# A Strassen down-projection over pairs of 512-token chunks

## The chip, the core and the metric

One NeuronCore of one Trainium2 chip runs the whole kernel. The metric is the device time of one launch in microseconds (us), the median of three runs. Engines are named as in the profile: PE (TensorE, matrix multiply; PEld is its loading of weights), DVE (VectorE), ACT (ScalarE), POOL (GpSimd) and SP (SyncE, which only issues DMAs). Each engine runs its own instructions in the order in which the program lists them (the schedule is manual for all five), and waits on semaphores for the others.

## What is computed

```python
def _attn_ref(u, v, z):                      # u, v: 8 x 3008 x 256; z: 8 x 3008 x 64
    scores = (1.0 / S) * np.matmul(z, z.transpose(0, 2, 1))
    attn = np.maximum(scores, 0.0) ** 2
    return (u * np.matmul(attn, v)).astype(np.float32)

def _moe_ref(x, w_in, w_out):                # x: 24064 x 256, the rows of the above
    h = x @ w_in                             # 256 x 2048
    g = h * (1.0 / (1.0 + np.exp(-1.702 * h)))
    return (g @ w_out).astype(np.float32)    # 2048 x 256
```

An attention without softmax, gated by u, and then a feed-forward layer: an up-projection to 2048, a Gelu by sigmoid, a down-projection to 256.

## The kernel before

The batch loop has eight rounds. In each, the 3008 tokens form six chunks: five of 512, and a last one of 448. Of two successive batches the even one keeps only 384 tokens of its last chunk for the feed-forward, and its other 64 join the odd one's, which is then 512 wide (`blocks`).

**Attention.** For each query chunk `i`, `attend` yields some 47 steps; each is a pair of 64-row matmuls of 512 columns (or one of 128 rows), which accumulate `V` times the squared scores in two PSUM banks (L367). Between steps `take` emits score matmuls (L235), an ACT Relu (L256) and a DVE square into a tile of tag `a` (26 buffers, L270) for a later chunk; during the last query chunk these belong to the next batch. Some squares are also transposed by DMA on SP (`turn_unit`, L298) into tiles of tag `tt` (14 buffers). Those of the next batch's first chunk are put off in the list `late`. When a query chunk is done, DVE multiplies by `u` and leaves `XT`, 256 features by 512 tokens in float16.

**Up-projection.** `up_group(b, q)` makes 256 of the 2048 hidden rows for one chunk: four matmuls of 512 columns (L408) into an `hg` tile (two PSUM buffers), a Gelu on ACT (L416) into `gf` (two buffers), and a scaling into float16 `GT` (tag `tt`) on DVE (L420), or, where `q % 8` is 1, 3 or 5 and `q` is 16 or more, on ACT (L418). A chunk has eight groups, a batch 48. The first 16 are emitted between the steps of a query chunk (the fifth; in the last batch the sixth), the other 32 after attention, each followed by one product of the down-projection. The products that are left (10 or 11) follow without up groups.

**Down-projection.** It is a Strassen-Winograd product within a chunk. The left matrix is `GT`, split by hidden rows (0 to 1023 and 1024 to 2047) and by tokens (even and odd blocks of 128): a11, a12 are the even blocks, a21, a22 the odd ones. The right matrix is `w_out`, split into four, with its sums t1 to t4n made once on DVE. The left sums S1 = a21 + a22, S2 = S1 - a11, S3 = a11 - a21 (in place of a21), S4 = a12 - S2 are made on DVE (L479 to L488); they wait in the list `SUMS`, of which each up group, after its scaling, emits one (two if more than eight wait). `product` emits one of seven products: eight matmuls of 256 columns (L532). There are three PSUM banks for a chunk, of the four of tag `ps1`: P1, P6, P7 and P4 add up in the first, P5 and P3 in the second, P2 has the third. What is read from a bank before the next product adds into it goes to `y`, either as an ACT copy (L549) or as a DVE addition (L553):

```python
lst += [(k, "P1")] + ([(k - 1, "P4"), (k - 1, "P3")] if k else []) + one   # one: P6 P5 P7 P2
...
copy = {"P1": (0, 0), "P6": (0, 1), "P7": (1, 1), "P4": (1, 0)}
outs = {"P2": (0, 0, "P2"), "P7": (1, 1, "P5"), "P3": (0, 1, "P5")}
```

Where a chunk has only 384 tokens, its Strassen part is 256 of them, so its matmuls have 128 columns, and the last 128 tokens are done by plain matmuls (`odd_block`, L506). In the last two chunks of the last batch `rows(b, k)` swaps the operands, so that tokens come out as rows (L535).

**Store.** When a chunk is done, `store` transposes `y` on DVE (L589) into `yo` (one buffer) and SP issues four DMAs (L599). The last two chunks of a batch are stored during the next one (`LAST2`). `y` has two buffers.

**Weights of the first layer.** In batch 0, `w_in` is loaded in four quarters by POOL (`load_w`) and cast by ACT (`cast_w`, L452) at places given by the tables `LOADW` and `CASTW`: keys are (query chunk, step), values the quarter. Quarter k holds up groups 2k and 2k + 1.

Of the kernel before, what the change touches and what calls it, by code (L numbers as in the profile page):

```python
# [9 lines left out]
F32 = mybir.dt.float32  # L10
F16 = mybir.dt.float16
P = 128
# [3 lines left out]
def kernel(  # L16
# [13 lines left out]
    AF = mybir.ActivationFunctionType  # L30
    ALU = mybir.AluOpType

    B, S, D = u.shape
# [20 lines left out]
    FSC = csc * csc * float(S) * float(S)  # L54
# [23 lines left out]
    late, LATE = [], []  # L78
# [316 lines left out]
    GT, Y = {}, {}  # L395

    def blocks(b):

        return [(i, CH if i < NCH - 1 or b % 2 else LFULL) for i in range(NCH)]

    def up_group(b, q):
        k, fg = divmod(q, NFG)
        i, n = blocks(b)[k]
        hg = ps2.tile([P, FFG, CH], F32, name="hg", tag="ps2")
        for e in range(FFG):
            ff = fg * FFG + e
            for c in range(NCC):
                pe.matmul(  # L408
                    hg[:, e, :n], W1[:, c, ff * P:(ff + 1) * P], XT[b, i][:, c, :n],
                    start=(c == 0), stop=(c == NCC - 1),  # L410
                )
        if fg % 2 == 0:
            GT[b, k, fg // 2] = pa.tile([P, CB, CH], F16, name="gt", tag="tt", bufs=14)
        g = GT[b, k, fg // 2][:, (fg % 2) * FFG:(fg % 2 + 1) * FFG, :n]
        gf = pw.tile([P, FFG, CH], F32, name="gf", tag="gf")
        act.activation(gf[:, :, :n], hg[:, :, :n], AF.Gelu_apprx_sigmoid, scale=1.0 / FSC)  # L416
        if q >= LAGY and q % 8 in (1, 3, 5):
            act.activation(g, gf[:, :, :n], AF.Copy, scale=FSC)  # L418
        else:
            dve.tensor_scalar(g, gf[:, :, :n], FSC, None, ALU.mult)  # L420
        for s_ in [SUMS.pop(0) for _ in range(min(len(SUMS), 1 + (len(SUMS) > 8)))]:
            s_()
        if fg in (NFG - 3, NFG - 1):
            SUMS.extend(left_sums(b, k, fg == NFG - 1))


# [11 lines left out]

    def load_w(k):

        if k < 2:
            hold = const.tile([P, 1], F16, name=f"hold{k}")
            pool.tensor_copy(hold, XT[0, k + 1][:, 0, :1])
# [46 lines left out]
    def products(b):  # L490

        lst = []
        for k in range(NCH):
            one = [(k, "P6"), (k, "P5"), (k, "P7"), (k, "P2")]
            if blocks(b)[k][1] < CH:
                one.insert(0, (k, "odd"))
            lst += [(k, "P1")] + ([(k - 1, "P4"), (k - 1, "P3")] if k else []) + one
        return lst + [(k, "P4"), (k, "P3")]

    def odd_block(b, k):  # L500

        s = blocks(b)[k][1] // P - 1
        yp = ps1.tile([P, NCC, P], F32, name="yp", tag="ps1")
        for c in range(NCC):
            for ff in range(NFF):
                pe.matmul(  # L506
                    yp[:, c, :], W2K[:, ff, c], GT[b, k, ff // CB][:, ff % CB, s * P:(s + 1) * P],
                    start=c == 0 and ff == 0, stop=ff == NFF - 1, skip_group_check=True,
                )
        act.activation(Y[b, k][:, :, s * P:(s + 1) * P], yp, AF.Copy, scale=1.0 / FSC)  # L510

    def product(b, k, name):
        if name == "odd":
            odd_block(b, k)
            return
        mm = pairs(b, k)
        right = {
            "P1": W2K[:, LO, 0], "P2": W2K[:, HI, 0], "P3": W2K[:, HI, 1], "P4": WT[:, 3],
            "P5": WT[:, 0], "P6": WT[:, 1], "P7": WT[:, 2],
        }[name]  # L520
        if name in ("P1", "P2", "P5"):
            ST[b, k, "bank" + name] = ps1.tile([P, 2, P], F32, name="st", tag="ps1")
        bank = ST[b, k, "bank" + {"P6": "P1", "P7": "P1", "P4": "P1", "P3": "P5"}.get(name, name)][:, :mm]
        for ff in range(NFF // 2):
            h, f = divmod(ff, CB)
            lhs = {
                "P1": lambda: left(b, k, h, 0), "P2": lambda: left(b, k, h + 2, 0),
                "P4": lambda: left(b, k, h + 2, 1),
            }.get(name) or (lambda: ST[b, k, {"P3": "S4", "P5": "S1", "P6": "S2", "P7": "S3"}[name], h])
            first, last = name in ("P1", "P2", "P5") and ff == 0, ff == NFF // 2 - 1  # L530
            if not rows(b, k):
                pe.matmul(bank, right[:, ff], lhs()[:, f], start=first, stop=last, skip_group_check=True)  # L532
                continue
            for m in range(mm):
                pe.matmul(  # L535
                    bank[:, m], lhs()[:, f, m], right[:, ff],
                    start=first and m == 0, stop=last, skip_group_check=True,
                )
        if name == "P1":
            Y[b, k] = pw.tile([P, NCC, CH], F32, name="y", tag="y")  # L540

        if rows(b, k):
            y = Y[b, k].rearrange("p e x -> p (e x)").rearrange("p (o m t k) -> p k m o t", o=2, t=P, k=NCC)
        else:
            y = Y[b, k].rearrange("p k (m o t) -> p k m o t", o=2, t=P)[:, :, :mm]
        copy = {"P1": (0, 0), "P6": (0, 1), "P7": (1, 1), "P4": (1, 0)}
        if name in copy:
            o, c = copy[name]
            act.activation(y[:, c, :, o], bank, AF.Copy, scale=1.0 / FSC)  # L549
        outs = {"P2": (0, 0, "P2"), "P7": (1, 1, "P5"), "P3": (0, 1, "P5")}  # L550
        if name in outs:
            o, c, x = outs[name]
            dve.scalar_tensor_tensor(  # L553
                y[:, c, :, o], ST[b, k, "bank" + x][:, :mm], 1.0 / FSC, y[:, c, :, o], ALU.mult, ALU.add,
            )
        if rows(b, k):
            if name in ("P4", "P3"):
                store_rows(b, k, name == "P4")
        elif name == "P3" and k > NCH - 3 and b < B - 1:
            LAST2.append(lambda: store(b, k))  # L560
        elif name == "P3":
            store(b, k)
# [21 lines left out]
    def store(b, k):  # L584

        i, n = blocks(b)[k]
        r0, m = b * S + i * CH, n // QW
        yo = pw.tile([P, CH // QW, QW, NCC], F32, name="yo", tag="yo", bufs=1)
        dve.transpose(  # L589
            yo[:, :m].rearrange("p q c k -> p q k c"), Y[b, k][:, :, :n].rearrange("p k (q t) -> p q k t", t=QW),  # L590
        )
        parts = [(r0, 0, n)]
        if n > S - i * CH:
            full = S0 - i * CH
            parts = [(r0, 0, full)] + [((b - h) * S + S0, full + h * SREM, SREM) for h in range(2)]
# [11 lines left out]
    def pieces(b, i):  # L607
# [22 lines left out]
    LOAD0 = {(1, 14): 2, (2, 12): 3, (2, NJ + 20): 4, (4, 8): 5}  # L630
    TURN = {(1, NJ + 4): 2, (2, NJ + 4): 3, (4, NJ + 4): 4, (5, 8): 5}
    LOADW = {
        (2, 16): 0, (3, 0): 1, (3, 9): 2, (3, 41): 3, (4, 28): 4, (4, 34): 5, (4, 40): 6, (5, 0): 7,
    }
    CASTW = {(3, 8): 0, (3, 40): 1, (4, 8): 2, (4, 14): 3}
    LOAD = {(3, NJ + 20): 4, (4, NJ + 5): 5}

    FIRST_ZT, FIRST_CAST = {12: 4, 20: 5}, {5: 4, 13: 5}
# [46 lines left out]
    for b in range(B):  # L685
# [47 lines left out]
        for q in range(head, nup):  # L733
            if more and q in (head + 14, head + 20):
                k = int(q == head + 20)
                turn_u(b + 1, k)
                load_u(b + 1, k + 2)
            up_group(b, q)
            if b == 0 and q == head + 3:
                wsums.pop(0)()  # L740
            product(b, *prods.pop(0))
            if q >= 30 and q % 2 and late:
                late.pop(0)[1]()
        steps = [lambda kp=kp: product(b, *kp) for kp in prods]
# [41 lines left out]
```

## Time and profile before

| what | value |
|---|---|
| runs | 1179.65 us median (1179.23 to 1181.85) |
| span of the profiled execution, first to last instruction | 1177.7 us (its time around the span is not given) |
| PE busy | 1171.1 us, 9284 matmuls |
| PE weight loads busy | 670.1 us, 9284 loads |
| DVE, ACT busy | 870.9 us, 849.7 us |
| POOL busy | 208.0 us |
| matmuls of the up-projection (L408) | 1536 |
| matmuls of the Strassen products (L532; L535) | 2576; 224 |
| plain matmuls of the odd blocks (L506) | 128 |

The profile is of one execution. A group's line gives the line of the code, the engine, the operation, the tiles written and read, the shape, the count, then busy time and the mean duration of one in ns, then the idle time of the engine before them and what ended it. Matmuls are pipelined: the duration of one runs from its start to the end of its results, and the next starts earlier. A timeline's line has start and duration in us; an x8 after it means that eight like instructions are merged.

### The profile page before, as it was taken

What the parts mean: (1) busy time and instruction counts of PE and PEld (TensorE: products, weight loads), DVE (VectorE), ACT (ScalarE), POOL (GpSimd) and SP (SyncE); (2) the same over time, 40 slices, a digit from 0 to 9 for tenths busy, and PEclk for the clock granted to TensorE, in tenths of its full rate; (3) what the DMA queues carried; (4) which work ended last, traced back from release to release, by engine and by line L of the source; (5) the groups of instructions that cost most, each with busy time, mean ns of one, the idle gap of its engine ahead of it and who ended that gap; (6) DMA issues with size and microseconds to landing.
All of it is one profiled execution on the core that took longest, in us unless ns stands there. A gap on an engine that the chain in (4) does not pass through costs nothing.

```text
span 1177.7 us, 23588 instructions
## 1 busy us (share of the span) xinstructions
PE 1171.1 (99%) x9284; PEld 670.1 (57%) x9284; DVE 870.9 (74%) x1455; ACT 849.7 (72%) x1033; POOL 208.0 (18%) x294
## 2 busy tenths in 40 slices
PE   9999999999999999999999999999999999999998
PEld 3546764466644675446654467544674446744566
DVE  6788875778757786587875878658786587764776
ACT  7888874688646887478864787657876578772785
POOL 3033101231012310133101430014200241001000
PEclk9999999999999999999999999999999999999999
DMA  9998679866797678966779668795678955797023
GB/s 221 207 141 123 134 114 160 94 108 135 117 148 97 108 137 129 146 97 94 147 121 146 103 93 155 125 151 92 98 134 142 136 104 97 126 157 129 1 37 73
DMA packets 459039, 143.65 MB, mean 122 GB/s; under 512 B 424624, under 2 KB 453040, under 8 KB 458928
## 3 DMA queue, kind: packets, MB, share of 16 engines
q1 hardware_dynamic: 402464, 102.36, 53.1%
q0 software_dynamic: 55104, 38.49, 21.5%
q8 instruction: 72, 1.18, 0.4%
q10 hardware_dynamic: 1360, 1.31, 0.3%
q14 instruction: 39, 0.32, 0.1%
HBM read 60.29 MB, written 24.64 MB: 72 GB/s over the span
## 4 chain that ended last, share of the span: by engine, by line
PE 99%; ACT 1%; DVE 0%; issue 0%
PE o L367 40%; PE hg L408 28%; PE st L532 23%; PE sc L235 6%; PE st L535 1%; PE yp L506 1%; PE w L99 0%; ACT rl L256 0%; ACT W L452 0%; ACT gf L416 0%; PE zp L135 0%; ACT ZT L143 0%; DVE a L270 0%; DVE zst L128 0%; DVE y L553 0%
## 5 line engine op out<-in xcount | busy, mean ns | idle before, releaser
L416 ACT ACTIVATE gf<-hg 128x1024 f32<-128x1024 f32 (+1 forms) x384 | 385.4, 1004 | 113.7 <-PE hg L408 98.7
L256 ACT ACTIVATE rl<-sc 128x1024 f16<-128x1024 f32 (+1 forms) x301 | 287.4, 993 | 144.6 <-PE sc L235 100.4
L367 PEld LDWEIGHTS <-V 64*128 64x128 f16 (+1 forms) x4098 | 219.7, 94 | 251.4 <-issue 9.3
L408 PE MATMUL hg<-xt,W 128*128 128x512 f16 (+1 forms) x1408 | 354.6, 374 | 0.2
L367 PE MATMUL o<-a,V 64*128 64x512 f16 (+3 forms) x2278 | 296.1, 368 | 0.3 <-DVE a L270 0.3
L420 DVE TENSOR_SCALAR gt<-gf 128x1024 f16<-128x1024 f32 (+1 forms) x288 | 200.2, 695 | 114.0 <-ACT gf L416 113.5
L270 DVE TENSOR_TENSOR a<-rl 128x1024 f16<-128x1024 f16 (+1 forms) x266 | 178.3, 674 | 112.0 <-ACT rl L256 110.0
L195 POOL DMA_DIRECT2D uq<-in_u_dram x168 | 110.7, 666 | 738.4 <-PE sc L235 529.0
L367 PE MATMUL o<-tt,V 64*128 64x512 f16 (+1 forms) x1518 | 232.5, 377 | 0.0
L408 PEld LDWEIGHTS <-W 128*128 128x128 f16 x1536 | 149.4, 98 | 125.5 <-issue 2.6
L532 PEld LDWEIGHTS <-WT 128*128 128x128 f16 x1472 | 139.1, 98 | 45.1
L532 PEld LDWEIGHTS <-W 128*128 128x128 f16 x1104 | 104.7, 98 | 32.2
L235 PE MATMUL sc<-ZT 64*128 64x512 f16 (+3 forms) x688 | 115.6, 356 | 0.6 <-ACT ZT L143 0.3
L418 ACT ACTIVATE gt<-gf 128x1024 f16<-128x1024 f32 (+1 forms) x96 | 98.9, 1030 | 3.0
L549 ACT ACTIVATE y<-st 128x256 f32<-128x256 f32 x192 | 70.7, 368 | 35.6 <-PE st L532 29.0
L532 PE MATMUL st<-gt,WT 128*128 128x256 f16 (+1 forms) x736 | 91.9, 268 | 0.0
L532 PE MATMUL st<-gt,W 128*128 128x256 f16 (+1 forms) x736 | 90.8, 268 | 0.0
L532 PE MATMUL st<-s,WT 128*128 128x256 f16 (+1 forms) x736 | 90.8, 268 | 0.0
L553 DVE SCALAR_TENSOR_TENSOR y<-st,y 128x256 f32<-128x256 f32 (+1 forms) x144 | 57.7, 408 | 24.6 <-ACT y L549 11.5
L384 DVE TENSOR_TENSOR xt<-o,ut 128x512 f16<-128x512 f32 x80 | 51.4, 683 | 28.5 <-PE o L367 28.5
L486 DVE TENSOR_TENSOR s<-s,gt 128x1024 f16<-128x1024 f16 (+1 forms) x96 | 65.6, 683 | 1.1
L484 DVE TENSOR_TENSOR s<-gt 128x1024 f16<-128x1024 f16 (+1 forms) x96 | 64.7, 674 | 0.0
(59 smaller groups left out, 670.3 us busy)
## 6 DMA issues: line engine op xcount, KB each, us to landing
out_dram<-yo SPq DMA_DIRECT2D x156, 128.0 KB, 2.8
uq<-in_u_dram POOLq DMA_DIRECT2D x140, 128.0 KB, 3.3
V<-in_v_dram POOLq DMA_DIRECT2D x35, 256.0 KB, 6.3
tt<-a SPq DMA_TRANSPOSE x232, 3.4
uq<-in_u_dram POOLq DMA_DIRECT2D x28, 112.0 KB, 4.5
out_dram<-yo SPq DMA_DIRECT2D x28, 96.0 KB, 7.1
uq<-in_u_dram SPq DMA_DIRECT2D x20, 128.0 KB, 4.2
wst<-in_moe_w_in_dram POOLq DMA_DIRECT2D x4, 512.0 KB, 5.8
```

What stands on the lines that cost most here:

```text
L195: eng.dma_start(uq[k * QW:(k + 1) * QW, :n // QW].rearrange("t q c k -> t q (c k)"), src[:, :, cs])
L235: pe.matmul(sc[:, r, :q1 - q0], zt[h, 2 * kp + r, :], zt[h].rearrange("d n p -> d (n p)")[:, q0:q1], start=True, stop=True,)
L256: act.activation(rl[:, :, :n], sc[:, :, :n], AF.Relu, scale=csc)
L270: dve.tensor_tensor(a[:, :, :n], rl[:, :, :n], rl[:, :, :n], ALU.mult)
L367: ins = pe.matmul(acc[c][:, :n], V16[b][h, j].rearrange("p (c k) -> p k c", k=NCC)[:, c], weights(b, i, j)[h], start=(k, m) == first[c], s ...
L408: pe.matmul(hg[:, e, :n], W1[:, c, ff * P:(ff + 1) * P], XT[b, i][:, c, :n], start=(c == 0), stop=(c == NCC - 1),)
L416: act.activation(gf[:, :, :n], hg[:, :, :n], AF.Gelu_apprx_sigmoid, scale=1.0 / FSC)
L418: act.activation(g, gf[:, :, :n], AF.Copy, scale=FSC)
L420: dve.tensor_scalar(g, gf[:, :, :n], FSC, None, ALU.mult)
L486: dve.tensor_tensor(s_, ST[b, k, "S1", h], a11, ALU.subtract)
L532: pe.matmul(bank, right[:, ff], lhs()[:, f], start=first, stop=last, skip_group_check=True)
L549: act.activation(y[:, c, :, o], bank, AF.Copy, scale=1.0 / FSC)
```

## The change

The Strassen split by tokens now takes two neighbouring chunks: a11, a12 are chunk 2s, a21, a22 chunk 2s + 1. All three pairs are formed in batches 0 to 6; in batch 7 the third pair is left as it was, with `product` (`paired`). In the third pair of an even batch the width `w` is 384, and the 128 tokens that chunk 4 has beyond that go to `odd_block`.

- The up groups of a pair are interleaved: 16 groups in the order of `TILES`, each hidden group first for one chunk, then for the other. A `GT` tile holds one hidden group of both chunks.
- `pair_product` emits a product in two halves of four matmuls of up to 512 columns, one half after each up group. P5 is now copied by ACT and P7 added by DVE.
- The order of the halves is a list; for the third pair another one. 32 halves stand after up groups as 32 products did, and 10 or 11 steps follow.
- `pair_sum` makes the left sums by hidden group. S1, S2, S3 of a group are put into `SUMS` two groups after its a11, S4 three groups after.
- Stores: chunk 2s when P2 is done, chunk 2s + 1 two steps after P4 (`AFTER`); those of the third pair go to `LAST2`.
- `late` is emitted from q = 44 on at each group, no longer from q = 30 at each odd one.
- Quarters 1 and 2 of `w_in` change places in `LOADW` and `CASTW`.

```diff
+    TILES = (0, 4, 1, 5, 2, 6, 3, 7)
     def up_group(b, q):
-        k, fg = divmod(q, NFG)
+        s, r = divmod(q, 2 * NFG)
+        pair = paired(b, s)
+        if pair:
+            fg, e = TILES[r // 2], r % 2
+            if fg >= NFG // 2:
+                e = 1 - e
+            k = 2 * s + e
...
+            if r % 2 == 0:
+                GT[b, s, fg, "pair"] = pa.tile([P, FFG, 2, CH], F16, name="gt", tag="tt", bufs=14)
+            g = GT[b, s, fg, "pair"][:, :, k % 2, :n]
...
+        if pair:
+            some = {2: ("S1", "S2", "S3"), 3: ("S4",)}.get(r % 4, ())
+            SUMS.extend([lambda m=m, fg=fg: pair_sum(b, s, fg - NFG // 2, m) for m in some])
...
+            if s < NCH // 2 - 1:
+                order = ["P1", "P1", "P5", "P5", "P6", "P6", "P3", "P3", "P7", "P7", "P2", "P2", "P4", "P4"]
+            else:
+                order = ["P1", "P1", "P5", "P2", "P5", "P2", "P6", "P6", "P3", "P3", "P7", "P7", "P4", "P4"]
+                if blocks(b)[2 * s + 1][1] < CH:
+                    order[6:6] = ["odd"]
...
+        for ff in range(half * NFF // 4, (half + 1) * NFF // 4):
+            m, f = divmod(ff, FFG)
+            while name in form and (b, s, form[name], m) not in ST:
+                SUMS.pop(0)()
+            lhs = pair_part(b, s, raw[name])(m) if name in raw else ST[b, s, form[name], m]
+            pe.matmul(
+                bank, right[:, ff], lhs[:, f], start=new and ff == 0, stop=ff == NFF // 2 - 1, skip_group_check=True,
+            )
...
+        copy = {"P1": (0, 0), "P5": (1, 1), "P6": (0, 1), "P4": (1, 0)}
+        outs = {"P3": (0, 1), "P7": (1, 1), "P2": (0, 0)}
...
+        elif name == "P2" and not last:
+            store(b, 2 * s)
+        elif name == "P4":
+            AFTER.append([2, lambda: store(b, 2 * s + 1)])
...
-        (2, 16): 0, (3, 0): 1, (3, 9): 2, (3, 41): 3, (4, 28): 4, (4, 34): 5, (4, 40): 6, (5, 0): 7,
+        (2, 16): 0, (3, 0): 2, (3, 9): 1, (3, 41): 3, (4, 28): 4, (4, 34): 5, (4, 40): 6, (5, 0): 7,
...
-    CASTW = {(3, 8): 0, (3, 40): 1, (4, 8): 2, (4, 14): 3}
+    CASTW = {(3, 8): 0, (3, 40): 2, (4, 8): 1, (4, 14): 3}
...
-            if q >= 30 and q % 2 and late:
+            if q >= 44 and late:
                 late.pop(0)[1]()
```

More of the change, by code (lines that the diff above doesn't have):

```diff
@@ L399, in blocks, with paired @@
         return [(i, CH if i < NCH - 1 or b % 2 else LFULL) for i in range(NCH)]
+    def paired(b, s):
+        return b < B - 1 or s < NCH // 2 - 1
+    TILES = (0, 4, 1, 5, 2, 6, 3, 7)
     def up_group(b, q):
-        k, fg = divmod(q, NFG)
+        s, r = divmod(q, 2 * NFG)
[6 more added lines that the diff above has]
+        else:
+            k, fg = divmod(q, NFG)
         i, n = blocks(b)[k]
@@ L411, in up_group @@
                 )
-        if fg % 2 == 0:
-            GT[b, k, fg // 2] = pa.tile([P, CB, CH], F16, name="gt", tag="tt", bufs=14)
-        g = GT[b, k, fg // 2][:, (fg % 2) * FFG:(fg % 2 + 1) * FFG, :n]
+        if pair:
+            if r % 2 == 0:
+                GT[b, s, fg, "pair"] = pa.tile([P, FFG, 2, CH], F16, name="gt", tag="tt", bufs=14)
+            g = GT[b, s, fg, "pair"][:, :, k % 2, :n]
+        else:
+            if fg % 2 == 0:
+                GT[b, k, fg // 2] = pa.tile([P, CB, CH], F16, name="gt", tag="tt", bufs=14)
+            g = GT[b, k, fg // 2][:, (fg % 2) * FFG:(fg % 2 + 1) * FFG, :n]
         gf = pw.tile([P, FFG, CH], F32, name="gf", tag="gf")
@@ L422, in up_group @@
             s_()
-        if fg in (NFG - 3, NFG - 1):
+        if pair:
+            some = {2: ("S1", "S2", "S3"), 3: ("S4",)}.get(r % 4, ())
+            SUMS.extend([lambda m=m, fg=fg: pair_sum(b, s, fg - NFG // 2, m) for m in some])
+        elif fg in (NFG - 3, NFG - 1):
             SUMS.extend(left_sums(b, k, fg == NFG - 1))
@@ L439, in load_w @@
     def load_w(k):
-        if k < 2:
+        if k in (0, 2):
             hold = const.tile([P, 1], F16, name=f"hold{k}")
-            pool.tensor_copy(hold, XT[0, k + 1][:, 0, :1])
+            pool.tensor_copy(hold, XT[0, 1 + k // 2][:, 0, :1])
         if k < 4:
@@ L492, in products, with pair_part, pair_sum, odd_block @@
         lst = []
[L493 to L502, printed above, removed]
+        for s in range(NCH // 2):
+            if not paired(b, s):
+                continue
+            if s < NCH // 2 - 1:
+                order = ["P1", "P1", "P5", "P5", "P6", "P6", "P3", "P3", "P7", "P7", "P2", "P2", "P4", "P4"]
+            else:
+                order = ["P1", "P1", "P5", "P2", "P5", "P2", "P6", "P6", "P3", "P3", "P7", "P7", "P4", "P4"]
+                if blocks(b)[2 * s + 1][1] < CH:
+                    order[6:6] = ["odd"]
+            lst += [lambda s=s, m=m, h=order[:x].count(m): pair_product(b, s, m, h) for x, m in enumerate(order)]
+        if not paired(b, NCH // 2 - 1):
+            k = NCH - 2
+            names = [(k, m) for m in ("P1", "P6", "P5", "P7", "P2")] + [(k + 1, "P1"), (k, "P4"), (k, "P3")]
+            names += [(k + 1, m) for m in ("P6", "P5", "P7", "P2", "P4", "P3")]
+            lst += [lambda k=k, m=m: product(b, k, m) for k, m in names]
+        return lst
+    def pair_part(b, s, name):
+        f, e = {"a11": (0, 0), "a12": (1, 0), "a21": (0, 1), "a22": (1, 1)}[name]
+        w = blocks(b)[2 * s + 1][1]
+        return lambda m: GT[b, s, f * NFG // 2 + m, "pair"][:, :, e, :w]
+    def pair_sum(b, s, m, name):
+        a11, a12, a21, a22 = (pair_part(b, s, x)(m) for x in ("a11", "a12", "a21", "a22"))
+        if name == "S3":
+            ST[b, s, name, m] = a21
+            dve.tensor_tensor(a21, a11, a21, ALU.subtract)
+            return
+        s_ = pa.tile([P, FFG, CH], F16, name="s", tag="a", bufs=26)
+        s_ = ST[b, s, name, m] = s_[:, :, :blocks(b)[2 * s + 1][1]]
+        if name == "S1":
+            dve.tensor_tensor(s_, a21, a22, ALU.add)
+        elif name == "S2":
+            dve.tensor_tensor(s_, ST[b, s, "S1", m], a11, ALU.subtract)
+        else:
+            dve.tensor_tensor(s_, a12, ST[b, s, "S2", m], ALU.subtract)
+    def odd_block(b, s):
+        k, w = 2 * s, blocks(b)[2 * s + 1][1]
         yp = ps1.tile([P, NCC, P], F32, name="yp", tag="ps1")
@@ L506, in odd_block @@
                 pe.matmul(
-                    yp[:, c, :], W2K[:, ff, c], GT[b, k, ff // CB][:, ff % CB, s * P:(s + 1) * P],
+                    yp[:, c, :], W2K[:, ff, c], GT[b, s, ff // FFG, "pair"][:, ff % FFG, 0, w:w + P],
                     start=c == 0 and ff == 0, stop=ff == NFF - 1, skip_group_check=True,
                 )
-        act.activation(Y[b, k][:, :, s * P:(s + 1) * P], yp, AF.Copy, scale=1.0 / FSC)
+        act.activation(Y[b, k][:, :, w:w + P], yp, AF.Copy, scale=1.0 / FSC)
@@ new lines, in pair_product @@
+    def pair_product(b, s, name, half):
+        if name == "odd":
+            odd_block(b, s)
+            return
+        w = blocks(b)[2 * s + 1][1]
+        right = {
+            "P1": W2K[:, LO, 0], "P2": W2K[:, HI, 0], "P3": W2K[:, HI, 1], "P4": WT[:, 3],
+            "P5": WT[:, 0], "P6": WT[:, 1], "P7": WT[:, 2],
+        }[name]
+        raw = {"P1": "a11", "P2": "a12", "P4": "a22"}
+        form = {"P3": "S4", "P5": "S1", "P6": "S2", "P7": "S3"}
+        new = name in ("P1", "P2", "P5")
+        if new and half == 0:
+            ST[b, s, "bank" + name] = ps1.tile([P, CH], F32, name="st", tag="ps1")
+        bank = ST[b, s, "bank" + {"P6": "P1", "P7": "P1", "P4": "P1", "P3": "P5"}.get(name, name)][:, :w]
+        for ff in range(half * NFF // 4, (half + 1) * NFF // 4):
[6 more added lines that the diff above has]
+            )
+        if half == 0:
+            return
+        for e, at in ((0, "P1"), (1, "P5")):
+            if name == at:
+                Y[b, 2 * s + e] = pw.tile([P, NCC, CH], F32, name="y", tag="y")
+        copy = {"P1": (0, 0), "P5": (1, 1), "P6": (0, 1), "P4": (1, 0)}
+        outs = {"P3": (0, 1), "P7": (1, 1), "P2": (0, 0)}
+        e, c = copy.get(name) or outs[name]
+        y = Y[b, 2 * s + e][:, c, :w]
+        if name in copy:
+            act.activation(y, bank, AF.Copy, scale=1.0 / FSC)
+        else:
+            dve.scalar_tensor_tensor(y, bank, 1.0 / FSC, y, ALU.mult, ALU.add)
+        last = s == NCH // 2 - 1
+        if name == "P4" and last:
+            LAST2.extend([lambda: store(b, 2 * s), lambda: store(b, 2 * s + 1)])
+        elif name == "P2" and not last:
+            store(b, 2 * s)
+        elif name == "P4":
+            AFTER.append([2, lambda: store(b, 2 * s + 1)])
@@ L512, in product @@
+    AFTER = []
     def product(b, k, name):
-        if name == "odd":
-            odd_block(b, k)
-            return
         mm = pairs(b, k)
@@ L740 @@
                 wsums.pop(0)()
-            product(b, *prods.pop(0))
-            if q >= 30 and q % 2 and late:
+            prods.pop(0)()
+            for a_ in AFTER:
+                a_[0] -= 1
+            while AFTER and AFTER[0][0] < 0:
+                AFTER.pop(0)[1]()
+            if q >= 44 and late:
                 late.pop(0)[1]()
-        steps = [lambda kp=kp: product(b, *kp) for kp in prods]
+        steps = prods
         for step in steps:
```

## The prediction

> **What bounds the kernel now.** I read the page first: busy times, the clock row, the chain.
>
> ```profile
> PE 1171.1 (99%) x9284; PEld 670.1 (57%) x9284; DVE 870.9 (74%) x1455; ACT 849.7 (72%) x1033; POOL 208.0 (18%) x294
> ...
> PEclk9999999999999999999999999999999999999999
> ...
> PE 99%; ACT 1%; DVE 0%; issue 0%
> ```
>
> TensorE (PE) is idle for 6.6 us of a span of 1177.7 us, at full clock, and the chain is PE nearly from end to end. PE waits for almost nobody, so there are two ways to change the time: matmul time taken away, or a wait of PE that was not there.
>
> Second, the groups by shape, for the price of a matmul.
>
> ```profile
> L408 PE MATMUL hg<-xt,W 128*128 128x512 f16 x1280 | 328.6, 379 | 0.2
> L532 PE MATMUL st<-gt,WT 128*128 128x256 f16 x672 | 87.1, 273 | 0.0
> L506 PE MATMUL yp<-gt,W 128*128 128x128 f16 x128 | 7.8, 219 | 0.0
> ```
>
> The mean of one (379, 273, 219 ns) is its latency, not its price, since matmuls overlap. The price is the distance between neighbouring starts in the trace: 215.9 ns for 512 columns (mean of 1056), 109.2 ns for 256 (2100), 55.8 for 128, 162.5 for 384 (L408 on the short chunk). So a column costs 0.417 ns and a matmul some 2.5 ns besides. A 512-column matmul ends 379 - 216 = 0.163 us after the next one could start; 384 columns give the same 0.163.
>
> Third, the timeline of the last up groups of a batch (b = 3); q counts up groups, q = 44 starts at 579.84, q = 47 at 585.05. Columns: start, duration.
>
> ```profile
> 578.10 1.03 PE L408 MATMUL hg<-xo,W 128*128 128x512 f16 x4
> 579.22 1.02 ACT L416 ACTIVATE gf<-hg 128x1024 f32<-128x1024 f32 x1 [0.23 <-PE hg L408]
> 579.84 1.03 PE L408 MATMUL hg<-xo,W 128*128 128x512 f16 x4
> 580.28 1.06 ACT L418 ACTIVATE gt<-gf 128x1024 f16<-128x1024 f32 x1
> 580.70 1.04 PE L532 MATMUL st<-s,W 128*128 128x256 f16 x8
> 581.24 0.37 ACT L549 ACTIVATE y<-st 128x256 f32<-128x256 f32 x1
> 581.51 1.02 ACT L416 ACTIVATE gf<-hg 128x1024 f32<-128x1024 f32 x1
> 582.55 0.69 DVE L420 TENSOR_SCALAR gt<-gf 128x1024 f16<-128x1024 f32 x1 [1.91 <-ACT gf L416]
> ...
> 583.75 1.06 ACT L418 ACTIVATE gt<-gf 128x1024 f16<-128x1024 f32 x1
> ...
> 585.91 1.04 PE L532 MATMUL st<-gt,WT 128*128 128x256 f16 x8
> 586.17 1.02 ACT L416 ACTIVATE gf<-hg 128x1024 f32<-128x1024 f32 x1 [0.17 <-PE hg L408]
> 587.24 0.69 DVE L420 TENSOR_SCALAR gt<-gf 128x1024 f16<-128x1024 f32 x1
> 587.84 0.69 DVE L486 TENSOR_TENSOR s<-s,gt 128x1024 f16<-128x1024 f16 x1
> ```
>
> The reader is to see how late a result is. From the slot after up group 44 (580.70) to its scaled tile (582.55 + 0.69 = 583.24) pass 2.54 us, because ACT first did step 43's Gelu, copy and y copy. From the slot after group 47 (585.91) to the end of the sum that follows it on DVE (588.53) pass 2.62 us. Before, no product needs these results at once. A waiting matmul starts 0.05 us after its releaser (447.06 + 0.28 to 447.39 below); DVE starts 0.04 us after a matmul's end (594.64 + 1.04 to 595.72).
>
> **What goes.** Per pair of chunks 7 x 8 matmuls of 512 columns replace 7 x 16 of 256: the columns are the same, half the matmuls go. 23 pairs are formed (three in batches 0 to 6, two in batch 7), so 1288 matmuls go. In 19 pairs 2 x 109.2 - 215.9 = 2.5 ns, in the four short ones (w = 384) 109.2 + 55.8 - 162.5 = 2.5 ns: 1288 x 2.5 = **-3.2 us**. In the four even batches two 128-wide products wait for an ACT copy of their bank:
>
> ```profile
> 447.06 0.28 ACT L549 ACTIVATE y<-st 128x128 f32<-128x128 f32 x1
> 447.39 0.61 PE L532 MATMUL st<-gt,WT 128*128 128x128 f16 x8
> ```
>
> each 0.08 us; P6 and P7 now have other products between: 4 x 2 x 0.08 = **-0.7 us**. In batch 0 two up groups (68.10, 71.19 us) wait 0.28 us each for the cast of a W1 quarter emitted just before; in the new order quarters 1 and 3 are first read at q = 8 and 10 instead of 4 and 6: **-0.6 us**. Together -4.5 us.
>
> **What is moved at no cost.** In the steady steps ACT's worst two steps (Gelu 1.06, copy 0.96, y copy of 512 columns 0.49, Gelu 0.90, start to start) make 3.41 us against PE's 2 x 1.73 = 3.45; without that 0.04 ACT falls behind, with the two hg buffers as cover (a Gelu may end 0.86 + 0.86 + 0.86 = 2.6 us after its group before PE stalls). DVE does the same sums and half as many additions of twice the width. Stores come in twos, four steps (6.9 us) apart; DVE's transpose 1.27, SP's four issues 2.18 and the landing 2.8 make 6.3, so yo is free again; otherwise DVE is late by under 1 us before sums needed 3 steps later. The late transposes pass SP's stores of q = 45 and run to the end of the batch, 1.6 us each; the first is read by the next batch's first query chunk at its last keys, 5 us on. Tiles: at most 13 of 14 tt live by the new order; two more sum tiles live through query chunk 5, where at least 3 of 26 were free. The moved loads and casts are as many on POOL and ACT.
>
> **What is added: three waits of PE at the end of batches 0 to 6.** Before the last pair an operand is ready steps ahead. The last pair starts at q = 44, and PE, in order, catches up with ACT and DVE.
>
> *P1, second half, q = 45.* Its last two matmuls read a11 of group 3, made at q = 44. Ready: 2.54 + 0.05, plus 0.23 because the y copy of step 43 is 512 wide (shortest start to start 0.49 against 0.26): 2.82 us. PE arrives after a half product, an up group and two matmuls: 0.86 + 0.86 + 0.43 = 2.16; in even batches, 384 wide, 0.65 + 0.65 + 0.33 = 1.63. Wait 0.66, even 1.19. Ends: with ACT on time (step 47: 587.24 + 0.69 + 0.05 - 585.91 = 2.07) it is 0 or 0.44; were the tile awaited whole, with the copy of q = 45 (583.75 + 1.06 + 0.05 - 580.70 = 4.16), 2.0 or 2.5. I take the row that it copies. Queued behind: up group 46, whose Gelu only gets later.
>
> *P5, second half, the first step after q = 47.* Its last two matmuls read S1 of group 3, which is popped at q = 47 behind that group's scaling on DVE: 2.62 + 0.05 = 2.67. PE arrives after one half of P2 and two matmuls: 0.86 + 0.43 = 1.30; even 0.65 + 0.33 = 0.98, with a sum 0.13 shorter. Wait 1.37, even 1.56; 0.3 to either side, which a Gelu started later or earlier can move. Queued behind: the rest of the products and the next batch's scores.
>
> *P4 right after P7, in one bank.* P4 adds into the bank that DVE must first read for y(1,1), and in the last pair P2 no longer stands between. For the width of that read:
>
> ```profile
> L384 DVE TENSOR_TENSOR xt<-o,ut 128x512 f16<-128x512 f32 x80 | 51.4, 683 | 28.5 <-PE o L367 28.5
> ...
> L386 DVE TENSOR_TENSOR xt<-o,ut 128x384 f16<-128x384 f32 x8 | 4.4, 549 | 0.0
> ```
>
> 0.16 + 0.04 + 0.68 + 0.05 = 0.93; even 0.16 + 0.04 + 0.55 + 0.05 = 0.80. Ends: 0.67 with the 0.42 of a 256-wide addition, 1.6 with another DVE operation ahead. Behind it: the next batch's scores.
>
> Odd batches (1, 3, 5): 0.66 + 1.37 + 0.93 = 2.96; even (0, 2, 4, 6): 1.19 + 1.56 + 0.80 = 3.55. 3 x 2.96 + 4 x 3.55 = **+23.1 us**. Sum: 23.1 - 4.5 = +18.6. The working is made on the profiled execution, whose span is 1177.7 us; the unprofiled runs, which take in what lies around the span, are 1.5 to 4.1 us above it (1179.23 to 1181.85), so I add the difference to their median, 1179.65: **1198.2 us**.
>
> A rule speaks against all this. The Trainium skill, "TensorE: Matmul & The Clock Gate", section "Back-to-back issue gap", says that in a stream of weight loads and matmuls 512 columns are sustained at about 131 ns each and 128 at 81; by that a 512-wide product would gain tens of us. This trace has 215.9 and 55.8 ns, so I leave it.
>
> **Rivals.** *Only the bank wait is real:* the operand waits vanish if sums and scaled tiles come a step earlier than I read. For: before, PE never waits for a sum. Against: the order on DVE is fixed, and 588.53 stands in the trace. Then 3 x 0.93 + 4 x 0.80 = 6.0 less 4.5: 1181.2. *More waits:* ACT's 0.04 of room in the odd steps with a copy and a y copy is not kept, or P1 waits for the whole tile: 1.3 us more per batch, 7 x 1.3 = 9, to 1207; for it, ACT already starts late by 1 us after such steps; against, hg has two buffers. *Faster:* each removed matmul also removes a weight load of 98 ns; were these not hidden, each worth over (23.1 - 1.3) / 1288 = 17 ns decides; at 25 ns the time is 1179.65 + 21.8 - 32.2 = 1169. Against: 128-wide matmuls start every 55.8 ns, each with such a load. That the columns were fewer than I count is excluded by the shapes.
>
> **Chances.** Forecast 0.74, more waits 0.13, only the bank wait 0.07, faster 0.06. All waits at their low ends make 3 x 1.7 + 4 x 2.4 = 15 and 1190; their high ends together 1215, which is unlikely for all at once; the range is 1188 to 1210. A measurement of this kernel tells about 0.2% (2.4 us) from no change, so 1181.2 counts as no change: faster 0.06, same 0.07, slower 0.87.
>
> **What would show it.** PE's idle time rises from 6.6 to some 25 us (each wait less its 0.16 overlap), nearly all at 21 places: product matmuls released by a DVE scaling, a DVE sum S1 and a DVE addition into y, in batches 0 to 6 and not in 7. Product matmuls stand 215.9 ns apart; weight loads fall by 1288. The casts' waits in batch 0 are gone. I am wrong if those 21 places show no gaps, or if steps q = 16 to 43 show some.

## The result

The changed kernel takes **1201.13 us** (median of 5 runs, 1200.80 to 1202.51), the kernel before 1179.57 us (1179.23 to 1181.85) beside it: a ratio of 1.0183, with a 95% interval of 1.0171 to 1.0196. That is 21.6 us slower, where +18.6 and 1198.2 us were forecast; it lies inside the range (1188 to 1210). The profiled execution is the slowest of the five (1202.51 us); its span is 1200.7 us against 1177.7: +23.0.

The page of the changed kernel (busy times, clock row, chain by engine):

```profile
PE 1171.5 (98%) x7996; PEld 576.7 (48%) x7996; DVE 862.8 (72%) x1386; ACT 838.1 (70%) x941; POOL 214.4 (18%) x294
...
PEclk9999999999999999999999999999999999999999
...
PE 91%; ACT 3%; issue 2%; DVE 2%; DMA 1%; ACTq 0%; POOL 0%; POOLq 0%
```

The clock is full, as before. 1288 matmuls and as many weight loads are gone (9284 to 7996). PE's busy time is the same to 0.4 us although its columns are the same and 1288 x 2.5 ns went: busy time here includes the tails of matmuls that precede a gap. PE's idle time is 1200.7 - 1171.5 = 29.2 us, where it was 6.6. The chain, which was PE to 99%, now passes through ACT and DVE.

The groups by shape show whom PE waits for (busy, mean of one in ns, then idle before them and its releaser):

```profile
L422 PE MATMUL hg<-xt,W 128*128 128x512 f16 x1280 | 328.5, 379 | 1.1 <-ACT gf L435 1.1
...
L585 PE MATMUL st<-gt,WT 128*128 128x512 f16 x304 | 77.0, 379 | 2.3 <-DVE y L600 2.3
...
L585 PE MATMUL st<-s,WT 128*128 128x384 f16 x64 | 13.0, 326 | 5.6 <-DVE s L547 5.6
...
L559 PE MATMUL yp<-gt,W 128*128 128x128 f16 x128 | 7.8, 219 | 0.0
```

Matmuls are as long as before (379 and 219 ns); what is new is idle time ahead of product matmuls (L585). PE's waits in the same trace, by line and releaser: us in total, how often, the longest.

```profile
PE st L585 <- DVE s L547: 9.2, 7, 1.4
PE st L585 <- DVE gt L439: 5.6, 7, 1.0
PE st L585 <- DVE y L600: 4.9, 7, 0.8
PE sc L235 <- ACT rl L256: 1.5, 2, 1.2
PE w L99 <- DVE nil L75: 1.2, 1, 1.2
PE hg L422 <- ACT gf L435: 1.1, 1, 1.1
PE st L631 <- ACT y L645: 0.4, 1, 0.4
```

The first three lines are the three forecast waits, seven times each: once in each of the batches 0 to 6. Idle time is counted from the modelled end of the matmul before, so it is 0.16 us less than the time lost: 9.2 + 5.6 + 4.9 = 19.7 idle, and 19.7 + 21 x 0.163 = 23.1 lost. The starts give 23.2.

**The three places in batch 3**, from the timeline of the changed kernel (start, duration). First P1's second half, in step 45:

```profile
592.38 1.03 PE L422 MATMUL hg<-xo,W 128*128 128x512 f16 x4
592.55 1.98 ACT L435 ACTIVATE gf<-hg 128x1024 f32<-128x1024 f32 x2
...
593.25 0.59 PE L585 MATMUL st<-gt,W 128*128 128x512 f16 x2
593.59 0.69 DVE L439 TENSOR_SCALAR gt<-gf 128x1024 f16<-128x1024 f32 x1 [2.00 <-ACT gf L435]
...
594.34 0.38 PE L585 MATMUL st<-gt,W 128*128 128x512 f16 x1 [0.50 <-DVE gt L439]
```

Two matmuls run at 593.25; the third could start 2 x 0.216 later, at 593.68, but its operand's scaling ends at 593.59 + 0.69 = 594.28. It starts at 594.34: 0.66 lost. Then P5's second half, after group 47:

```profile
598.22 0.59 PE L585 MATMUL st<-s,WT 128*128 128x512 f16 x2
...
598.68 0.70 DVE L439 TENSOR_SCALAR gt<-gf 128x1024 f16<-128x1024 f32 x1 [0.34 <-ACT gf L435]
...
599.29 0.69 DVE L547 TENSOR_TENSOR s<-gt 128x1024 f16<-128x1024 f16 x1
...
600.02 0.59 PE L585 MATMUL st<-s,WT 128*128 128x512 f16 x2 [1.21 <-DVE s L547]
```

S1 of group 3 stands behind the scaling of group 47 on DVE and ends at 599.98: 600.02 - (598.22 + 0.43) = 1.37 lost. Last P4 behind P7:

```profile
604.77 1.89 PE L585 MATMUL st<-gt,WT 128*128 128x512 f16 x8
...
606.70 0.69 DVE L600 SCALAR_TENSOR_TENSOR y<-st,y 128x512 f32<-128x512 f32 x1 [0.96 <-PE st L585]
607.44 0.38 PE L585 MATMUL st<-gt,WT 128*128 128x512 f16 x1 [0.78 <-DVE y L600]
```

The eight matmuls (P7's two halves) end at 606.66, DVE reads P7's bank until 607.39, and P4 starts at 607.44 instead of 606.50: 0.94 lost.

**The account of the 23.0 us**, from matmul starts in both traces. A loss by starts is the distance between two neighbouring starts less the price of the first matmul (215.9 ns at 512 columns); unlike idle time it holds the 0.16 us as well.

| what | us |
|---|---|
| three waits, batches 0 to 6 | +23.2 |
| fewer matmuls (1288 x 2.5 ns) | -3.2 |
| waits for bank copies in even batches | -0.7 |
| batch 7: P6 of chunk 4 for a copy (below) | +0.6 |
| next batches' scores for a Relu (below) | +0.6 |
| batch 0, late landings: 3.3 lost (1.3 and 2.0), before 0.6 (casts) | +2.7 |
| sum | +23.2 |

Three entries were not in the forecast. In batch 7 the pair that is left as it was has P6 directly after P1, without the products of the chunk before that once stood between, and P1's copy waits on ACT behind a wide copy and a Gelu:

```profile
1181.16 0.58 ACT L598 ACTIVATE y<-st 128x512 f32<-128x512 f32 x1
...
1181.64 1.01 ACT L435 ACTIVATE gf<-hg 128x1024 f32<-128x1024 f32 x1
...
1182.55 0.40 ACT L645 ACTIVATE y<-st 128x256 f32<-128x256 f32 x1
...
1183.00 1.05 PE L631 MATMUL st<-WT,s 128*128 128x128 f16 x16 [0.44 <-ACT y L645]
```

After each of the batches 0 to 6 the next batch's first Relu stands behind P4's copy, which is now 512 wide (609.37 + 0.60 us in batch 3), so the third score group starts 0.14 us late in odd batches and 0.04 in even ones: 3 x 0.143 + 4 x 0.036 = 0.57. No wait is listed for it, since it is shorter than the 0.16 of overlap. In batch 0 a load of a `w_in` quarter landed late, so its cast held up a Gelu (1.3 us), and a weight sum on DVE waited for `w_out` while squares stood behind it (2.0 us). That load of `w_out` was itself issued late, at 85.52 instead of 81.91 us: POOL, which issues it, had stood 7.24 us, where it was 3.92 before, at a late load of `z`.

```profile
71.41 1.06 ACT L474 ACTIVATE W<-wst 128x1024 f16<-128x1024 f32 x1 [1.29 <-DMA wst<-in_moe_w_in_dram]
...
94.04 1.23 DVE L480 TENSOR_TENSOR WT<-W 128x1024 f16<-128x1024 f16 x1 [2.78 <-DMA W<-in_moe_w_out_dram]
```

### The profile page after: what moved, and what is told of

Same layout as the page of the kernel before. It is cut to its first block, busy times and chain, and to the rows that moved or that the text cites. A ratio compares the mean times of both kernels' runs of the same rounds, so it can differ in the third digit from the quotient of the medians.

```text
span 1200.7 us, 20853 instructions
## 1 busy us (share of the span) xinstructions
PE 1171.5 (98%) x7996; PEld 576.7 (48%) x7996; DVE 862.8 (72%) x1386; ACT 838.1 (70%) x941; POOL 214.4 (18%) x294
## 4 chain that ended last, share of the span: by engine, by line
PE 91%; ACT 3%; issue 2%; DVE 2%; DMA 1%; ACTq 0%; POOL 0%; POOLq 0%
PE o L367 38%; PE hg L422 26%; PE st L585 21%; PE sc L235 5%; ACT gf L435 2%; DMA wst<-in_moe_w_in_dram 1%; PE st L631 1%; DVE gt L439 1%; PE yp L559 1%; ACT y L598 0%; DVE y L600 0%; ACT rl L256 0%; DVE s L547 0%; PE w L99 0%; DVE a L270 0%
## 5 line engine op out<-in xcount | busy, mean ns | idle before, releaser
L367 PEld LDWEIGHTS <-V 64*128 64x128 f16 (+1 forms) x4098 | 240.4, 94 | 230.6 <-issue 9.3
L195 POOL DMA_DIRECT2D uq<-in_u_dram x168 | 115.5, 695 | 749.0 <-PE sc L235 550.6
L422 PEld LDWEIGHTS <-W 128*128 128x128 f16 x1536 | 149.6, 98 | 177.2 <-issue 4.2
L585 PEld LDWEIGHTS <-WT 128*128 128x128 f16 x736 | 71.8, 98 | 94.2 <-issue 17.6
L585 PE MATMUL st<-s,WT 128*128 128x512 f16 (+1 forms) x368 | 91.0, 370 | 9.2 <-DVE s L547 9.2
L585 PE MATMUL st<-gt,W 128*128 128x512 f16 (+1 forms) x368 | 92.1, 370 | 5.6 <-DVE gt L439 5.6
L585 PE MATMUL st<-gt,WT 128*128 128x512 f16 (+1 forms) x368 | 88.7, 370 | 4.9 <-DVE y L600 4.9
L598 ACT ACTIVATE y<-st 128x512 f32<-128x512 f32 (+1 forms) x92 | 52.0, 565 | 56.2 <-PE st L585 56.2
L585 PEld LDWEIGHTS <-W 128*128 128x128 f16 x552 | 54.0, 98 | 66.8 <-issue 7.4
L600 DVE SCALAR_TENSOR_TENSOR y<-st,y 128x512 f32<-128x512 f32 (+1 forms) x69 | 45.9, 665 | 27.4 <-PE st L585 27.3
L542 DVE TENSOR_TENSOR gt<-gt 128x1024 f16<-128x1024 f16 (+1 forms) x92 | 62.6, 681 | 0.0
```

The costliest lines, as they stand in the source:

```text
L195: eng.dma_start(uq[k * QW:(k + 1) * QW, :n // QW].rearrange("t q c k -> t q (c k)"), src[:, :, cs])
L367: ins = pe.matmul(acc[c][:, :n], V16[b][h, j].rearrange("p (c k) -> p k c", k=NCC)[:, c], weights(b, i, j)[h], start=(k, m) == first[c], s ...
L422: pe.matmul(hg[:, e, :n], W1[:, c, ff * P:(ff + 1) * P], XT[b, i][:, c, :n], start=(c == 0), stop=(c == NCC - 1),)
L542: dve.tensor_tensor(a21, a11, a21, ALU.subtract)
L585: pe.matmul(bank, right[:, ff], lhs[:, f], start=new and ff == 0, stop=ff == NFF // 2 - 1, skip_group_check=True,)
```

## The experiments

The theory is that of the prediction: three separate waits, each from the order of the last pair (or from what ACT has queued ahead of one), at the prices above, and 2.5 ns saved per matmul. Rival A: ACT and DVE are late as a whole at the end of a batch, so that taking one wait away moves it to the next place. Rival B: the width itself costs or gains, so that the orders matter little. Ratios are against the kernel before, measured beside each with 15 runs (medians 1179.50 and 1179.66).

One execution differs from another most in batch 0. So for each kernel the table also has PE's idle time in the first 110 us, as the windows of its trace give it, and the span without it. Idle time is 0.16 us short for each gap, so half a us in the last column is not to be read.

| kernel | median us | ratio, interval | span | PE idle to 110 us | rest | rest - changed |
|---|---|---|---|---|---|---|
| before | 1179.57 | 1 | 1177.7 | 2.6 | 1175.1 | -20.7 |
| before again (n1) | 1181.10, one run | | 1179.2 | 3.6 | 1175.6 | -20.2 |
| changed | 1201.13 | 1.0183 (1.0171 to 1.0196) | 1200.7 | 4.9 | 1195.8 | 0 |
| e1 | 1196.24 | 1.0132 (1.0117 to 1.0148) | 1195.0 | 4.0 | 1191.0 | -4.8 |
| e2 | 1190.45 | 1.0092 (1.0079 to 1.0106) | 1190.4 | 4.5 | 1185.9 | -9.9 |
| e3 | 1195.90 | 1.0134 (1.0120 to 1.0148) | 1194.3 | 4.1 | 1190.2 | -5.6 |
| e4 | 1180.37 | 1.0013 (1.0001 to 1.0024) | 1178.6 | 3.6 | 1175.0 | -20.8 |
| e5 | 1203.56 | 1.0200 (1.0186 to 1.0213) | 1201.2 | 2.2 | 1199.0 | +3.2 |
| e6 | 1194.78 | 1.0130 (1.0114 to 1.0145) | 1193.0 | 2.4 | 1190.6 | -5.2 |
| e7 | 1179.87 | 0.9998 (0.9990 to 1.0007) | 1176.4 | 2.1 | 1174.3 | -21.5 |

### e1: P2's second half between P7 and P4

```diff
-                order = ["P1", "P1", "P5", "P2", "P5", "P2", "P6", "P6", "P3", "P3", "P7", "P7", "P4", "P4"]
+                order = ["P1", "P1", "P5", "P2", "P5", "P6", "P6", "P3", "P3", "P7", "P7", "P2", "P4", "P4"]
-                    order[6:6] = ["odd"]
+                    order[5:5] = ["odd"]
```

> The changed kernel, but in the last pair the second half of P2 stands between P7 and P4 (order P1 P1 P5 P2 P5 P6 P6 P3 P3 P7 P7 P2 P4 P4). Theory: each of the 21 waits costs what its own place shows, and they are independent. The wait of P4 for the bank (0.945 us in the three odd batches, 0.81 in the four even ones up to batch 6) shrinks by the half product that now covers it (0.86 and 0.65 us), to about 0.08 and 0.16 us: 5.2 us less than the changed kernel's 1201.1, so 1195.9, and the other two waits stay as long as they were. Rival (the waits pass on: PE only catches up with DVE, and what it doesn't wait for here it waits for a little later, in P4's second half or in the next batch's scores): less than 2 us, 1199 or more.

1196.24 us. PE's waits in e1:

```profile
PE st L585 <- DVE s L547: 9.2, 7, 1.4
PE st L585 <- DVE gt L439: 5.7, 7, 1.0
```

The third line of the changed kernel (DVE y L600: 4.9) is gone; the others are the same. By starts P4 still loses 0.08 us in odd batches and 0.16 in even ones (it lost 0.94 and 0.81), since P2's half (four matmuls, 0.86 us at 512 columns) is a little shorter than the turn of the bank (0.945). Product waits fall from 23.2 to 18.0 us; the rest of the span falls by 4.8.

### e2: P6 between P5's halves

```diff
-                order = ["P1", "P1", "P5", "P2", "P5", "P2", "P6", "P6", "P3", "P3", "P7", "P7", "P4", "P4"]
+                order = ["P1", "P1", "P5", "P2", "P6", "P2", "P5", "P6", "P3", "P3", "P7", "P7", "P4", "P4"]
-                    order[6:6] = ["odd"]
+                    order[5:5] = ["odd"]
```

> The changed kernel, but in the last pair the second half of P5 stands two half products later (order P1 P1 P5 P2 P6 P2 P5 P6 P3 P3 P7 P7 P4 P4). Theory: its wait for the sum S1 (1.37 us in odd, 1.55 us in even batches) goes, since PE arrives 1.7 us (1.3 and the odd block in even batches) later and the sum is not later than before: 3 x 1.37 + 4 x 1.55 = 10.3 us less, perhaps 0.2 us given back where P3 now follows the copy of P5's bank closely: 1191.0. Rival (the waits pass on): the half of P2 or of P6 that now comes earlier waits for the scaled tile or for S2 instead, and less than 5 us is won: 1196 or more.

1190.45 us. The waits in e2:

```profile
PE st L585 <- DVE gt L439: 5.7, 7, 1.0
PE st L585 <- DVE y L600: 4.9, 7, 0.8
```

The largest of the three is gone, and the other two stand as they were. Product waits: 13.3 us, 9.9 less than 23.2, which is what the rest of the span lost. P3 now waits 0.09 us for a copy in even batches, and no other product wait grew. One up group among the steps of attention waits 0.34 us for its Gelu in one batch; single gaps of this kind, up to 0.34 us, stand in some traces and not in others (e6 has one too).

### e3: P5's first half between P1's halves

```diff
-                order = ["P1", "P1", "P5", "P2", "P5", "P2", "P6", "P6", "P3", "P3", "P7", "P7", "P4", "P4"]
+                order = ["P1", "P5", "P1", "P2", "P5", "P2", "P6", "P6", "P3", "P3", "P7", "P7", "P4", "P4"]
```

> The changed kernel, but in the last pair the second half of P1 and the first of P5 change places (order P1 P5 P1 P2 P5 P2 P6 P6 P3 P3 P7 P7 P4 P4), so that the tile scaled at q = 44 is read at q = 46. Theory: P1's wait (0.665 us in odd, 1.20 us in even batches) goes and P5's wait stays as long as it was, since the sum that it waits for follows up group 47 at a fixed distance: 3 x 0.665 + 4 x 1.20 = 6.8 us less, 1194.3. Rival (the waits pass on, ACT and DVE are the limit of the last four up groups): P5's wait grows by what P1's loses, and less than 2 us is won: 1199 or more.

1195.90 us. P1's wait (5.6 us in the view) is gone. Two things grew in even batches: P5's wait from 1.55 to 1.67 us, and a new 0.147 us of up group 46 for a Gelu, because PE now comes there earlier. Product waits and this one make 17.5 us, 5.7 less than before the edit; the rest of the span lost 5.6. So 1.1 of the 6.8 us passed on, where the expectation had nothing.

### e4: all three at once

```diff
-                order = ["P1", "P1", "P5", "P2", "P5", "P2", "P6", "P6", "P3", "P3", "P7", "P7", "P4", "P4"]
+                order = ["P1", "P5", "P1", "P2", "P6", "P2", "P5", "P6", "P3", "P7", "P7", "P3", "P4", "P4"]
-                    order[6:6] = ["odd"]
+                    order[5:5] = ["odd"]
```

> The changed kernel with all three waits dealt with by order alone (last pair: P1 P5 P1 P2 P6 P2 P5 P6 P3 P7 P7 P3 P4 P4, the odd block after the first half of P6). Theory: of 23.2 us of waits about 1 us is left (0.08 us at P4 in odd batches, 0.16 us in even ones, 0.05 us at P3): 22 us less, 1179.1, the time of the kernel before within 0.3 per cent; so the 3.2 us of matmul time that was saved is eaten by something else, in batch 0 and 7. Rival (something besides the three waits is slower, such as the wider copies or the order of the up groups all along): 1183 or more.

1180.37 us (11 runs). Of 21.6 us, 20.8 are gone by an order of the same 14 half products. The same stretch of batch 3, in the timeline of e4:

```profile
590.59 1.03 PE L585 MATMUL st<-s,W 128*128 128x512 f16 x4
591.46 1.89 PE L585 MATMUL st<-gt,WT 128*128 128x512 f16 x8
593.18 1.03 PE L585 MATMUL st<-s,W 128*128 128x512 f16 x4
594.20 1.89 PE L585 MATMUL st<-gt,WT 128*128 128x512 f16 x8
```

Four matmuls take 0.86 us, so all follow without a gap, but for P4 at 594.20, which is 0.15 us late: P3's half covers 0.86 us of the bank's turn. In e1 the same cover left 0.08; here DVE began its read 0.10 us after P7's end, there 0.04, and why is not shown. Rival B falls: the widths are those of the changed kernel. Rival A falls as well: the waits do not gather elsewhere. What is left, by starts: P4 0.15 and 0.23 us, P3 0.09, an up group 0.15, the odd block up to 0.31 behind its operand, the scores, and batch 7's 0.6; some 4 us, about as much as the 3.9 saved.

### n1: the kernel before, unchanged

The changed kernel lost 3.3 us in batch 0. Is that of the change?

> The kernel before once more, for a second profile of batch 0. In the changed kernel and in four variants PE loses 1.4 to 3.3 us in batch 0 (between 60 and 100 us) to DMAs that land 2 to 3 us later than in the one profile of before. If that comes with the change (the order of the weight quarters), this profile shows, as the first did, no wait in batch 0 but the two of 0.28 us for the casts. If landings differ from execution to execution whatever the kernel, this profile may show such a wait too.

1181.10 us in one run, span 1179.2. Its waits:

```profile
PE hg L408 <- ACT W L452: 1.1, 1, 1.1
PE o L367 <- DMA tt<-a: 0.7, 1, 0.7
```

Neither is listed in the first profile of this same kernel, where by starts the casts cost two up groups 0.28 us each. The last `w_in` quarter landed 9.4 us after its issue (6.25 in the first profile, 9.57 in the changed kernel), and the cast behind it held PE up for 1.23 us; with the other cast (0.28) and a wait for a transpose (0.89) batch 0 lost 2.4. So late landings come without the change, and e5 and e6, whose program is that of the changed kernel in these first 100 us, lost 0.4 and 0.3 us there. DVE's wait for `w_out` at the weight sum is another matter: it stands in six of the seven traces of the new order in which that sum has its old place (1.0 to 2.8 us; in three of them PE loses over 1 us by it), and in neither trace of the kernel before. Whether the new order brings it was not tested. How much of the changed kernel's median is of this kind was not settled: without batch 0 the traces differ by 20.7 us, the medians by 21.6.

### e5: products in pieces of 256 columns

```diff
-            pe.matmul(
-                bank, right[:, ff], lhs[:, f], start=new and ff == 0, stop=ff == NFF // 2 - 1, skip_group_check=True,
-            )
+            for x in range(0, w, 2 * P):
+                pe.matmul(
+                    bank[:, x:min(x + 2 * P, w)], right[:, ff], lhs[:, f, x:min(x + 2 * P, w)],
+                    start=new and ff == 0 and x == 0, stop=ff == NFF // 2 - 1, skip_group_check=True,
+                )
```

> The changed kernel, order and all, but each Strassen matmul of 512 columns is emitted as two of 256 (of 384 as 256 and 128), as before the change; only the size of the matmul is undone. Theory: a matmul costs 2.5 ns beside its columns, so 1288 more of them cost 3.2 us: 1201.1 + 3.2 = 1204.3, with matmuls 109 ns apart and the 21 waits unchanged. Rival (the column count alone decides, the wider matmul is worth nothing): 1201.1. Rival (the halved weight loads matter): 1210 or more.

1203.56 us, 2.4 above the changed kernel; without batch 0 its span is 3.2 longer. The page of e5, first line:

```profile
PE 1174.8 (98%) x9284; PEld 693.3 (58%) x9284; DVE 863.5 (72%) x1386; ACT 838.7 (70%) x941; POOL 214.5 (18%) x294
```

The 1288 matmuls and 1288 weight loads are back, 693.3 - 576.7 = 116.6 us of weight loading more, and they cost 3.2 us: 2.5 ns each, as the starts say too (109.1 ns apart at 256 columns). The loads are hidden. The three waits are unchanged (22.9 us). This is the term of the sum that the change gains, measured by itself.

### e6: the scaling of step 43 on DVE

```diff
-        if q >= LAGY and q % 8 in (1, 3, 5):
+        if q >= LAGY and q % 8 in (1, 3, 5) and (q != 43 or not pair):
```

> The changed kernel, but at q = 43 of the paired batches the Gelu is scaled on DVE and not on ACT. Theory: P1's wait is ACT's delay, a Gelu that starts late because the step before had a Gelu, a copy and a y copy in a row. Without that copy the Gelu of q = 44 starts when its up group ends, the tile is ready 2.07 us after the group instead of 2.82, and P1's wait falls from 0.665 to 0 in odd and from 1.20 to 0.45 in even batches: 3 x 0.665 + 4 x 0.75 = 5.0 us less, 1196.1; the other two waits stay. Rival (DVE is the limit there, or P1 waits for the whole tile with the copy of q = 45): less than 1.5 us is won, 1199.6 or more.

1194.78 us. No product moved; only ACT's queue ahead of step 44's Gelu became shorter. P1 in the waits of e6 (it was 5.6, 7, 1.0):

```profile
PE st L585 <- DVE gt L439: 0.9, 4, 0.2
```

P1 waits no longer in odd batches, and 0.38 us instead of 1.20 in even ones. So the wait comes from what ACT has queued ahead of the Gelu, as the prediction read it, not from the scaling on DVE that releases it. P5 then waits 1.55 instead of 1.37 us in odd batches: of the 0.66 that P1 gave, 0.18 passed on, since S1 became ready only 0.48 earlier. Product waits are 18.5 us, 4.7 less.

### e7: the best that these point to

The order of e4, the scaling of e6, and in addition

```diff
-            names = [(k, m) for m in ("P1", "P6", "P5", "P7", "P2")] + [(k + 1, "P1"), (k, "P4"), (k, "P3")]
+            names = [(k, m) for m in ("P1", "P5", "P6", "P2", "P7")] + [(k + 1, "P1"), (k, "P4"), (k, "P3")]
...
-                if b == 0 and i == NCH - 1 and n in (8, 30, 42):
+                if b == 0 and i == NCH - 1 and n in (28, 36, 44):
```

for batch 7's P6, and for the weight sums of batch 0, which now come after `w_out` has landed.

> All that the runs so far suggest together: the order of e4_all, DVE scaling at q = 43, in batch 7 P5 between P1 and P6 and P2 between P6 and P7, and the sums of the second layer's weights 20 steps later (steps 28, 36 and 44 of the last query chunk of batch 0), so that DVE doesn't stand at them while that weight still loads. Theory: against e4_all's 1180.4 the wait of an up group for a Gelu in even batches goes (0.6 us in all), batch 7's wait for the copy of P1 (0.6 us), and what batch 0 loses in the squares behind the weight sums (1.4 us): about 2.5 us less, 1178, which would be below the kernel before by 0.1 per cent, inside what can be told. Rival (batch 0 waits elsewhere for its DMAs, and DVE is late with its extra scaling): 1180 or more.

1179.87 us (11 runs) against 1179.66 (15): no difference that can be told. The medians fell by 0.5 us from e4 to e7, not by the 2.5 expected. The profiled execution, with 1178.19 us, is the second fastest of the eleven (1178.07 to 1181.06); what the slower ones lose was not profiled. In the profiled execution the gap of batch 7 is gone, 0.1 us is lost in batch 0, and product waits are 1.75 us, the odd blocks 0.9, the scores 0.6: 3.3, against 3.9 saved. The rest of the span is 0.8 us under that of the kernel before. The change is worth that little even where nothing waits for long.

## Why the prediction was right, point by point

- **The price of a matmul** (-3.2): right. Product matmuls of 512 columns stand 215.9 ns apart, those of 384 columns 162.5, and e5 measures the 2.5 ns. The Trainium skill, "TensorE: Matmul & The Clock Gate", section "Back-to-back issue gap", gives columns / 2.4 + 2.5 ns for an isolated matmul and about 131 ns at 512 columns in a stream. In these traces the stream itself keeps to the isolated figure.
- **Bank copies in even batches** (-0.7): gone, as worked out.
- **Casts in batch 0** (-0.6): the step that was mis-sized. The first cast holds PE up no longer. The second waited for its load, which landed 3.3 us later than in the trace that the term was read from: 1.3 us lost. ACT runs its queue in order, so the Gelu behind the cast waits as well, however late the quarter itself is read. The weight sum behind `w_out` cost another 2.0, so batch 0 lost 3.3 us instead of 0.6. n1 shows late loads of `w_in` with the old order too, for 2.4 us; the wait at the weight sum was seen with the new order alone. The term was below what one execution can tell. (The two old waits stand at 68.59 and 71.69 us, half a us after the times that the prediction names.)
- **P1** (0.66 odd, 1.19 even): measured 0.665 and 1.196. e6 shows the cause, ACT's queue, and e3 the place.
- **P5** (1.37, 1.56): measured 1.37 and 1.554. e2 shows the place.
- **P4** (0.93, 0.80): measured 0.945 and 0.812. The read of a bank of known width between two matmuls was priced right from a row of another line (0.68). e1 shows the place.
- **Their sum** (+23.1): 23.2, in 21 places, none in batch 7. PE's idle time, forecast at 25, is 29.2: the unforeseen gaps of batch 0 and 7 make 2.8 of the difference. Another 1.3 is a slip of the forecast, which took the old waits off in full; the idle time of before holds only 0.24 us of them (the casts), since the copies' 0.08 us are shorter than the 0.16.
- **What moves at no cost:** right in steps 16 to 43, where no product waited. It missed two neighbours of the moved steps: batch 7's unpaired chunk, which lost the products that covered its copy (+0.6), and the Relu behind P4's wider copy (+0.6). Both are copies on ACT whose cover was not asked for one by one.
- **Rivals:** with only the bank wait it would have been 1181.2, but the operand waits are there. More waits: the tile is not awaited whole, and ACT kept its pace. Faster by unhidden weight loads: e5 brings 1288 of them back for 3.2 us.

The missing 2.9 us between 1198.2 and 1201.13 are thus 1.2 of unforeseen small gaps, and for the rest batch 0, as far as one trace for each kernel tells. In the traces themselves 4.4 are missing (23.0 against 18.6): 1.2, and 3.3 of batch 0.

## What to carry to other kernels

When products are made wider or moved nearer to their operands, work out for each the time from the last operand's start on its engine to its readiness, queue included, and set it against PE's arrival; a list of 14 places took 21 us here that a different order of the same list gives back. Put another accumulation between two that share a PSUM bank when one engine must read it in between: here the turn costs 0.94 us at 512 columns, and four 512-wide matmuls cover 0.86 of it. Before halving the number of matmuls at equal columns, ask what one costs beyond its columns: at 2.5 ns, 1288 of them are 3.2 us, which a single wait per batch outweighs.

## What the runs showed of the hardware

- **The same load lands at very different times.** A 512 KB quarter of `w_in`, issued at the same place of the program, landed after 5.8 to 9.6 us (the last quarter) and 6.8 to 12.0 us (the third that is issued) in the ten profiled executions. With the cast or the sum queued ahead of work that PE needs, that makes 0.1 to 3.3 us of one execution.
- **A PE gap shorter than a matmul's tail is not listed.** The scores' 0.14 us, e4's P4 at 0.15 us and e1's 0.08 us show only in the starts.
- **A doubled number of weight loads in the products** (e5) cost nothing that can be seen beside 2.5 ns per matmul.
